# The second token product of an attention and mixer kernel: u by columns at the end of the segment, with x and u turned by DMA

## The chip, the cores and the metric

The kernel runs on one core of a Trainium2 chip. The metric is the device time of one launch in microseconds; smaller is better. The core has five engines with a queue each: TensorE (PE in the profile, with PEld for its weight loads), VectorE (DVE), ScalarE (ACT), GpSimd (POOL) and SyncE (SP), which here only issues DMAs.

## The reference

Cosine attention over 8 batches, 12 heads, 448 positions and 64 columns a head, and then one block of a token and channel mixer on its output. In short (the maximum that is taken off the scores is left out):

```python
q_n = q / (norm(q) + 1e-6);  k_n = k / (norm(k) + 1e-6)
attn = softmax(q_n @ k_n.T / tau)            # per batch and head, 448 x 448
x = (attn @ v) -> (8, 448, 768)              # heads side by side
xt = x.transpose(0, 2, 1)
h = relu(xt @ w_tok1) @ w_tok2               # 448 -> 256 -> 448 positions
u = x + h.transpose(0, 2, 1)
out = u + relu(u @ w_ch1) @ w_ch2            # 768 -> 1536 -> 768 columns
```

## The kernel before, in words

Work goes by **pairs** of heads: 8 batches of 6 pairs make 48, numbered i. Pair i belongs to batch i // 6. Positions of a pair lie in blocks of 128 (448 is three and a half; the half block lies at the end in even batches and at the front in odd ones, with zeros for the other half), 128 columns of a pair beside each other.

The order of all instructions is written out by hand (`manual_schedule`): each engine runs its own list in program order. Pairs 0 to 6 have their own prologue. From pair 7 on the **main loop** runs one **segment** for each i. In a segment i, TensorE does in this order:

- `score(i, 0..2)`: q times k into the banks psS (L340); ScalarE takes the exponential into pt (L341);
- `pv_rest(i - 1)` (L362) and `pv(i - 1)` (L379): pt times v into two banks psO, one for each head; VectorE divides by the row sum and writes x (L382, L383);
- a **unit** of the channel mixer of the batch before: one series of six matmuls into psG (`m_ch1`, L431), which ScalarE turns into gt (L434), or one of twelve into psF (`m_ch2`, L446), to which VectorE adds u (ost, L450);
- `score_rest(i)`: the rest of the scores, psQ (L347);
- `tok2(i - 2)`: the second token product. Eight matmuls of 128 columns (L406) give psU with positions on the partitions, VectorE adds x and writes u (u16, L409), and `udma` turns u by a DMA into ut, columns on the partitions, for `m_ch1` (L415);
- in segments up to 10, `tpose(i + 1)`: q and k of the next pair turned on TensorE (L317, copied out at L319). From pair 12 on this is done two segments ahead by a DMA instead (`tpose_dma`, L325; the bound is `DMA_T0`);
- more units, as many as the list `queue` says are due (`due()`), the first of them with `wide`;
- `tok1(i - 1)`: the first token product into psR (L392); VectorE writes the maximum with 0 as rt (L395).

`side(i)` stands between, with the other engines' work: loads of q and k some seven pairs ahead, squares and casts on GpSimd, norms on ScalarE, scaling of q and k into kq on GpSimd (L293, L301), `tpose_dma(i + 2)`, and the load of v four pairs ahead. From pair 18 on norms are taken for three pairs together. SP's list has, for each segment: q, k (and every third one the rests kr of three pairs), q's and k's transposition, v (and vr), u's transposition, and the stores of the output rows from ost.

The eight accumulation banks are two pools. Pool `ps`, tag b, has two buffers of one bank: psO, psU, psR, psT, pst and units that are not wide take turns in it. Pool `ps2`, tag s, has three of two banks: psS, psQ and wide units. A buffer is handed out again in the order of the program, so an allocation waits for the readers of the one two before it (in ps).

Before the main loop GpSimd sets some buffers to zero, loads the token weights w1t and w2n by DMA (L182, L186) and lays w2n out as w2t (`place_w2`, L189).

After segment 47 come the last pv, two tok2, one tok1, and the units that are left.

Of the kernel before, what the change touches and what calls it, by code (L numbers as in the profile page):

```python
# [7 lines left out]
FP32 = mybir.dt.float32  # L8
FP16 = mybir.dt.float16
AF = mybir.ActivationFunctionType  # L10
ALU = mybir.AluOpType
# [11 lines left out]
def kernel(  # L23
# [12 lines left out]
    nc = tc.nc  # L36

    B, H, S, E = q.shape
# [3 lines left out]
    SC = 112  # L42
    NCH = S // SC
    DT = D // 128
    CT = C // 128
    TT = T // 128
    DH = 384
    NDH = D // DH
    NPAIR = H // 2
# [2 lines left out]
    NHALF = 2 * B  # L52
    inv_tau = 1.0 / float(tau)
    EPS_NORM = 1e-6
    DMA_T0 = 12
    OLD = 2 * NPAIR
    SINGLE = 3 * NPAIR

# [8 lines left out]
    QS = 2 * NCH  # L67
# [16 lines left out]
    cst = ctx.enter_context(tc.tile_pool(name="cst", bufs=1))  # L84
    qkv = ctx.enter_context(tc.tile_pool(name="qkv", bufs=7))
    nrm = ctx.enter_context(tc.tile_pool(name="nrm", bufs=3))
    att = ctx.enter_context(tc.tile_pool(name="att", bufs=4))
    mix = ctx.enter_context(tc.tile_pool(name="mix", bufs=2))
    outp = ctx.enter_context(tc.tile_pool(name="outp", bufs=3))
    ps = ctx.enter_context(tc.tile_pool(name="ps", bufs=2, space=bass.MemoryType.PSUM))  # L90
# [3 lines left out]
    pipe = {}  # L94
    ut = {}
# [53 lines left out]

    w1t = cst.tile([128, 5, T], FP16, name="w1t")  # L150
    w2n = outp.tile([128, TT, S], FP16, name="w2n", tag="ost")
    w2t = cst.tile([128, TT, S + 64], FP16, name="w2t")
    wc1t = cst.tile([128, DT, C], FP16, name="wc1t")
    wc2t = cst.tile([128, CT, D], FP16, name="wc2t")

# [11 lines left out]
        pts.append(pt)  # L167
    nc.gpsimd.memset(w1t[64:128, 3, :], 0.0)
    nc.gpsimd.memset(w1t[0:64, 4, :], 0.0)
    nc.gpsimd.memset(w2t[:, :, S:S + 64], 0.0)  # L170

    def weights_tok1():
        todo = []
# [12 lines left out]
        nc.gpsimd.dma_start(out=w2n[:], in_=moe_w_tok2.rearrange("(tt p) s -> p tt s", p=128))  # L186

    def place_w2():
        nc.gpsimd.tensor_copy(out=w2t[:, :, 0:S].rearrange("p t (c s) -> p t c s", c=NCH),  # L189
                              in_=w2n[:].rearrange("p t (s c) -> p t c s", c=NCH))  # L190

    def weights_ch1(i):
        cols, t = slice(768 * (i // 2), 768 * (i // 2) + 768), 3 * (i % 2)
# [3 lines left out]
    def weights_ch2(i):  # L197
        nc.gpsimd.dma_start(out=wc2t[:, 6 * i:6 * i + 6, :],
                            in_=moe_w_ch2[768 * i:768 * (i + 1)].rearrange("(t p) d -> p t d", p=128))
# [8 lines left out]
    nes = [cst.tile([128, 2 * QS, 2], FP32, name=f"ne{i}") for i in range(3)]  # L208
    for ne in nes:
        nc.vector.memset(ne[:, :, 1], EPS_NORM)  # L210
    for sq in sqs:
        nc.vector.memset(sq[96:128, KS:KS + QS].rearrange("p c e -> p (c e)"), 0.0)

# [38 lines left out]
    def sums_of(i):  # L252
        n, col, w = (-1 - i, 0, 1) if i < SINGLE else (i // HP, i % HP, HP)
        h = half.setdefault(n, {})
        if "ssq" not in h:
            tag = "" if w > 1 else "1"
            h["ssq"] = nrm.tile([128, w, 2 * QS], FP32, name=f"ssq_{i}", tag="ssq" + tag, bufs=4)
            h["rn"] = nrm.tile([128, w, 2 * QS], FP32, name=f"rn_{i}", tag="rn" + tag, bufs=4)
        return h, col

    def sums(i, a0=0, a1=2):
# [90 lines left out]
    def pv_rest(i):  # L352
        if old(i):
            return
        st = pipe[i]
        st["x"] = att.tile([128, 4, 128], FP16, name=f"x_{i}", tag="x", bufs=3)
        st["psO"] = [ps.tile([128, 4, E + 2], FP32, name=f"psO_{i}_{hh}", tag="b") for hh in range(2)]
        for m, lo in enumerate(windows(i // NPAIR)):
            for hh in range(2):
                hb = slice(hh * 64, hh * 64 + 64)  # L360
                at = 2 * S * KC + lo
                nc.tensor.matmul(st["psO"][hh][:, m, 0:E + 1], pts[i % 2][hb, at:at + 128],  # L362
                                 vts[(i // HP) % NV][hb, i % HP, 2 * KC, 0:E + 1], start=(m == 0), stop=False)

    def pv(i, hh):
        st = pipe[i]
        vt = vts[(i // HP) % NV]
        if old(i):
            if hh == 0:
                st["x"] = att.tile([128, 4, 128], FP16, name=f"x_{i}", tag="x", bufs=3)  # L370
            n, nch = SC, NCH
            psO = ps.tile([128, 4, E + 2], FP32, name=f"psO_{i}_{hh}", tag="b")
        else:
            n, nch = 128, KC
            psO = st["psO"][hh]
        for m, lo in enumerate(windows(i // NPAIR)):
            for c in range(nch):
                at = (2 * c + hh) * S + lo
                nc.tensor.matmul(psO[:, m, 0:E + 1], pts[i % 2][0:n, at:at + 128], vt[0:n, i % HP, nch * hh + c, 0:E + 1],  # L379
                                 start=(old(i) and c == 0), stop=(c == nch - 1 and (old(i) or m == 3)))  # L380
        rec = att.tile([128, 4], FP32, name=f"rec_{i}_{hh}", tag="rec")
        nc.vector.reciprocal(out=rec[:], in_=psO[:, :, E])  # L382
        nc.vector.tensor_tensor(out=st["x"][:, :, hh * E:(hh + 1) * E], in0=psO[:, :, 0:E],  # L383
                                in1=_bcast_free(rec[:], E), op=ALU.mult)

    def tok1(i, wide=False):
        st = pipe[i]
        w1 = (0, 1, 2, 3) if (i // NPAIR) % 2 == 0 else (4, 0, 1, 2)
        psR = (ps2 if wide else ps).tile([128, TT, 128], FP32, name=f"psR_{i}", tag="s" if wide else "b")
        for tt in range(TT):  # L390
            for m in range(4):
                nc.tensor.matmul(psR[:, tt], w1t[:, w1[m], tt * 128:(tt + 1) * 128], st["x"][:, m],  # L392
                                 start=(m == 0), stop=(m == 3))
        st["rt"] = att.tile([128, TT, 128], FP16, name=f"rt_{i}", tag="rt", bufs=2)
        nc.vector.tensor_scalar_max(out=st["rt"][:], in0=psR[:], scalar1=0.0)  # L395

    def tok2(i, pe=False, wide=False):
        st = pipe[i]
        b, pj = i // NPAIR, i % NPAIR
        if pj == 0:  # L400
            u16[b] = mix.tile([128, DT, 4, 128], FP16, name=f"u16_{b}", tag="u16", bufs=4)
            ut[b] = mix.tile([128, DT, 4, 128], FP16, name=f"ut_{b}", tag="ut")
        psU = (ps2 if wide else ps).tile([128, 4, 128], FP32, name=f"psU_{i}", tag="s" if wide else "b")
        for m, lo in enumerate(windows(b)):
            for tt in range(TT):
                nc.tensor.matmul(psU[:, m], w2t[:, tt, lo:lo + 128], st["rt"][:, tt],  # L406
                                 start=(tt == 0), stop=(tt == TT - 1))
        u = u16[b][:, pj]
        nc.vector.tensor_tensor(out=u, in0=psU[:], in1=st["x"][:], op=ALU.add)  # L409
        if not pe:  # L410
            udma(i)
# [72 lines left out]
    def unit(wide=False):  # L484
        if queue:
            t, fn = queue.pop(0)
            fn(wide)
            fed[0] -= t
# [14 lines left out]
    with tc.manual_schedule():  # L503
# [119 lines left out]
        def side(i):  # L623
            single = i + 2 < SINGLE
            n = 6 if i < 2 * NPAIR else 7
            for t in range(i + n, i + (8 if i == 2 * NPAIR - 1 else n + 1)):
                if t < NP_ALL:
                    load_qk(t)
            for t in SQ_AT.get(i, [i + 3 if single else i + 5]):
                if t < NP_ALL:  # L630
                    squares(t)
            cast_v(i)
            if i in (8, 10):
                weights_ch2((i - 8) // 2)
            if single:
                norms(i + 2, i + 3)
                norms(i + 2, i + 3, dve=True)
            elif i + 4 < NP_ALL:
                sums(i + 4)
                if (i + 4) % HP == 2:  # L640
                    norms(i + 2, i + 5, act=True)
            if i + 2 < NP_ALL:
                scaled(i + 2)
                if i + 2 >= DMA_T0:
                    tpose_dma(i + 2)
            if i + 4 < NP_ALL:
                load_v(i + 4)

        for i in range(NPAIR + 1, NP_ALL):
            b, pj = i // NPAIR, i % NPAIR  # L650
            for c in range(KC):
                score(i, c)
            pv_rest(i - 1)
            pv(i - 1, 0)
            pv(i - 1, 1)
            if i == NPAIR + 1:
                upose(NPAIR - 2)
                upose(NPAIR - 1)
                refill(0)
            elif pj == 2 and b > 1:  # L660
                refill(b - 1)
            side(i)
            fed[0] += fed[1]
            unit(True)
            if old(i):
                score(i, KC)
            else:
                score_rest(i)
            if i > NPAIR + 1:
                tok2(i - 2)  # L670
            if i + 1 < DMA_T0:
                tpose(i + 1)
            if due():
                unit(True)
            while due():
                unit()
            tok1(i - 1)
            if i + 2 < SINGLE:
                for t in SU_AT.get(i, [i + 3]):
                    sums(t)  # L680
        last = NP_ALL - 1
        pv_rest(last)
        pv(last, 0)
        pv(last, 1)
        tok2(last - 1)
        unit()
        tok1(last)
        unit()
        tok2(last)
        refill(B - 1)  # L690
# [37 lines left out]
```

## Time and profile before

| | |
|---|---|
| runs shown | 397.54 us median of 3 (396.83 to 399.86) |
| the profiled execution | 395.4 us |
| its span (first to last instruction) | 393.6 us |
| PE busy in the span | 375.2 us, 95% |
| ACT, POOL, DVE busy | 224.8, 236.0, 210.5 us |
| DMA queue of SP (q1) | 113104 packets, 67.6% of 16 engines' span |
| L406, psU, 384 matmuls | 29.4 us busy |
| L415, u's transposition | 45 issues, median 3.2 us to landing |
| L325, q's and k's transposition | 36 issues, median 3.4 us to landing |

Busy time of an engine says how long it had work, not whether anything waited for it; matmuls overlap, so their durations in rows add up to more than the time from one to the next. In rows of a timeline the columns are start and duration in us, engine, line and operation, output and inputs, shapes and count, and in brackets the idle time before and what ended it. SPq rows are issues by SP's queue: their duration is how long the queue was held, not the transfer. "Landing" is the transfer's end.

### The profile page before, as it was taken

What the parts mean: (1) busy time and instruction counts of PE and PEld (TensorE: products, weight loads), DVE (VectorE), ACT (ScalarE), POOL (GpSimd) and SP (SyncE); (2) the same over time, 40 slices, a digit from 0 to 9 for tenths busy, and PEclk for the clock granted to TensorE, in tenths of its full rate; (3) what the DMA queues carried; (4) which work ended last, traced back from release to release, by engine and by line L of the source; (5) the groups of instructions that cost most, each with busy time, mean ns of one, the idle gap of its engine ahead of it and who ended that gap; (6) DMA issues with size and microseconds to landing.
All of it is one profiled execution on the core that took longest, in us unless ns stands there. A gap on an engine that the chain in (4) does not pass through costs nothing.

```text
span 393.6 us, 10211 instructions
## 1 busy us (share of the span) xinstructions
PE 375.2 (95%) x4132; PEld 243.5 (62%) x4132; DVE 210.5 (53%) x469; ACT 224.8 (57%) x378; POOL 236.0 (60%) x383
## 2 busy tenths in 40 slices
PE   5899899899999999999999999999999999999994
PEld 5567566476556666667656666667666666655562
DVE  6889767567544574465534574456534653421031
ACT  5899578665574547764574547755575536411400
POOL 6999887889777592939587592949484630000000
PEclk9899999999999999999999999999999999999999
DMA  8999999989787778896897688686786384022022
GB/s 213 260 234 205 243 260 195 219 216 218 177 201 172 156 182 213 161 174 177 176 220 165 156 213 202 159 176 146 183 187 132 91 158 68 15 65 83 0 81 81
DMA packets 117951, 65.26 MB, mean 166 GB/s; under 512 B 75920, under 2 KB 114320, under 8 KB 117904
## 3 DMA queue, kind: packets, MB, share of 16 engines
q1 hardware_dynamic: 113104, 58.71, 67.6%
q0 software_dynamic: 4080, 5.21, 7.7%
q10 hardware_dynamic: 720, 0.69, 0.6%
q8 instruction: 32, 0.52, 0.6%
q14 instruction: 15, 0.12, 0.1%
HBM read 43.45 MB, written 11.01 MB: 138 GB/s over the span
## 4 chain that ended last, share of the span: by engine, by line
PE 79%; POOL 6%; ACT 5%; DVE 5%; issue 2%; DMA 1%; POOLq 0%
PE psF L446 26%; PE psG L431 26%; PE psO L379 8%; PE psS L340 6%; PE psU L406 5%; PE psR L392 4%; ACT pt L341 3%; POOL kq L293 2%; PE psQ L347 2%; POOL sq L241 1%; DVE ssq L264 1%; PE psO L362 1%; POOL w1t L182 1%; DVE ost L450 1%; DMA qk<-kq 1%
## 5 line engine op out<-in xcount | busy, mean ns | idle before, releaser
L341 ACT ACTIVATE pt<-psS 128x896 f16<-128x896 f32 (+1 forms) x156 | 132.5, 917 | 57.8 <-PE psS L340 57.6
L431 PE MATMUL psG<-ut,wc1t 128*128 128x448 f16 x576 | 116.8, 352 | 0.8 <-ACT gt L434 0.8
L446 PE MATMUL psF<-wc2t,gt 128*128 128x384 f16 x672 | 115.9, 326 | 0.2 <-ACT gt L434 0.2
L446 PEld LDWEIGHTS <-gt 128*128 128x128 f16 x672 | 63.6, 98 | 39.0 <-issue 0.3
L434 ACT ACTIVATE gt<-psG 128x448 f16<-128x448 f32 x96 | 51.3, 543 | 60.9 <-PE psG L431 60.9
L293 POOL TENSOR_TENSOR kq<-kf,rn 128x384 f16<-128x384 f32 (+1 forms) x47 | 42.3, 899 | 70.8 <-ACT rn L281 62.0
L431 PEld LDWEIGHTS <-wc1t 128*128 128x128 f16 x576 | 53.9, 98 | 45.4 <-issue 1.1
L450 DVE TENSOR_TENSOR ost<-psF,u 128x384 f32<-128x384 f32 (+1 forms) x64 | 35.5, 554 | 63.6 <-PE psF L446 62.3
L264 DVE TENSOR_REDUCE ssq<-sq 128x15 f32<-128x960 f32 (+2 forms) x49 | 55.7, 1140 | 3.0 <-ACT sq L239 2.9
L395 DVE TENSOR_SCALAR rt<-psR 128x256 f16<-128x256 f32 x48 | 20.2, 420 | 62.6 <-PE psR L392 62.5
L293 POOL TENSOR_TENSOR kq<-qf,rn 112x512 f16<-112x512 f32 x45 | 47.0, 1044 | 3.0
L379 PE MATMUL psO<-vt,pt 128*128 128x65 f16 (+1 forms) x1248 | 48.3, 193 | 0.0
L379 PEld LDWEIGHTS <-pt 128*128 128x128 f16 (+1 forms) x1248 | 42.2, 97 | 5.1 <-issue 1.9
L340 PE MATMUL psS<-qk 64*128 64x448 f16 x312 | 41.3, 358 | 3.5 <-DMA qk<-kq 2.1
L383 DVE TENSOR_TENSOR x<-psO,rec 128x256 f16<-128x256 f32 x96 | 40.8, 425 | 3.3
L241 POOL TENSOR_TENSOR sq<-kf 128x384 f32<-128x384 f32 (+1 forms) x46 | 40.1, 872 | 1.9 <-DVE ssq L264 1.9
L241 POOL TENSOR_TENSOR sq<-qf 112x512 f32<-112x512 f32 x39 | 40.5, 1039 | 0.0
L409 DVE TENSOR_TENSOR u<-psU,x 128x512 f16<-128x512 f32 x48 | 33.0, 688 | 6.0 <-PE psU L406 4.4
L382 DVE RECIPROCAL rec<-psO 128x4 f32<-128x4 f32 x96 | 16.9, 176 | 29.0 <-PE psO L379 29.0
L406 PEld LDWEIGHTS <-w2t 128*128 128x128 f16 x384 | 24.6, 98 | 10.4 <-issue 3.3
L406 PE MATMUL psU<-rt,w2t 128*128 128x128 f16 x384 | 29.4, 219 | 1.7 <-DVE rt L395 1.1
L392 PEld LDWEIGHTS <-w1t 128*128 128x128 f16 x384 | 25.0, 98 | 8.2 <-DVE x L383 1.2
(55 smaller groups left out, 262.2 us busy)
## 6 DMA issues: line engine op xcount, KB each, us to landing
qf<-in_q_dram SPq DMA_DIRECT2D x48, 224.0 KB, 3.9
kf<-in_k_dram SPq DMA_DIRECT2D x36, 192.0 KB, 3.4
vf<-in_v_dram SPq DMA_DIRECT2D x36, 192.0 KB, 3.2
vf<-in_v_dram SPq DMA_DIRECT2D x12, 224.0 KB, 7.8
out_dram<-ost SPq DMA_DIRECT2D x8, 336.0 KB, 3.1
wc1t<-in_moe_w_ch_dram POOLq DMA_DIRECT2D x4, 576.0 KB, 10.2
wc2t<-in_moe_w_ch_dram POOLq DMA_DIRECT2D x2, 1152.0 KB, 10.7
out_dram<-ost SPq DMA_DIRECT2D x8, 288.0 KB, 2.9
```

The source lines that it names most:

```text
L241: nc.gpsimd.tensor_mul(out=dst, in0=src, in1=src)
L264: nc.vector.tensor_reduce(out=h["ssq"][0:n, col, sl], in_=pipe[i]["sq"][0:n, sl], axis=AXX.X, op=ALU.add)
L293: eng.tensor_tensor(out=kq[0:p, a, 0:n].rearrange("p c g e -> p g c e"), in0=st["kq"[a]][:].rearrange("p (g c) e -> p g c e", g=2), in1=_b ...
L340: nc.tensor.matmul(psS[:, hh, 0:S], qk[hb, c * n:c * n + 128], qm[hb], start=True, stop=True)
L341: nc.scalar.activation(out=pts[i % 2][0:n, 2 * S * c:2 * S * (c + 1)].rearrange("p (h s) -> p h s", h=2), in_=psS[0:n, :, 0:S], func=AF.Ex ...
L379: nc.tensor.matmul(psO[:, m, 0:E + 1], pts[i % 2][0:n, at:at + 128], vt[0:n, i % HP, nch * hh + c, 0:E + 1], start=(old(i) and c == 0), st ...
L383: nc.vector.tensor_tensor(out=st["x"][:, :, hh * E:(hh + 1) * E], in0=psO[:, :, 0:E], in1=_bcast_free(rec[:], E), op=ALU.mult)
L392: nc.tensor.matmul(psR[:, tt], w1t[:, w1[m], tt * 128:(tt + 1) * 128], st["x"][:, m], start=(m == 0), stop=(m == 3))
L406: nc.tensor.matmul(psU[:, m], w2t[:, tt, lo:lo + 128], st["rt"][:, tt], start=(tt == 0), stop=(tt == TT - 1))
L431: nc.tensor.matmul(psG[:, 0:S], wc1t[:, dt, ct * 128:(ct + 1) * 128], ut[b][:, dt].rearrange("p m s -> p (m s)")[:, lo:lo + S], start=(dt ...
L434: nc.scalar.activation(out=gt[:, ct, (b % 2) * S:(b % 2 + 1) * S], in_=psG[:, 0:S], func=AF.Relu)
L446: nc.tensor.matmul(psF[:, 0:DH], gt[:, ct, lo:lo + 128], wc2t[:, ct, dh * DH:(dh + 1) * DH], start=(ct == 0), stop=(ct == CT - 1))
```

## The change

- From pair 12 (batch 2) on `tok2` has rt as the stationary operand and w2t as the moving one: two matmuls of 448 columns into psU, columns of u on the partitions. VectorE adds x in that layout and writes ut directly; a DMA turns ut into u16, which `m_ch2` adds.
- For that, x of each of these pairs is turned by a DMA too, `xdma`, into xt. It is issued on SP in the next segment, between the loads of q and k and q's and k's transposition.
- From segment 14 on `tok2(i - 2)` stands at the end of the segment, after the due units and ahead of `tok1(i - 1)`. After the last segment the order is xdma, a unit, tok1, tok2, two units, tok2.
- Pair 12's q and k are turned on TensorE in segment 11.
- ut becomes two fixed buffers, of which GpSimd zeroes a part once; w2t is 64 columns wider with a second small copy; x has two buffers where it had three, and the sums of squares and norms of three pairs have three where they had four.

```diff
-    DMA_T0 = 12
+    DMA_T0 = 13
...
-    w2t = cst.tile([128, TT, S + 64], FP16, name="w2t")
+    w2t = cst.tile([128, TT, S + 128], FP16, name="w2t")
...
-    nc.gpsimd.memset(w2t[:, :, S:S + 64], 0.0)
+    nc.gpsimd.memset(w2t[:, :, S + 64:S + 128], 0.0)
...
+        w2c = w2n[:].rearrange("p t (s c) -> p t c s", c=NCH)
+        nc.gpsimd.tensor_copy(out=w2t[:, :, 64:S + 64].rearrange("p t (c s) -> p t c s", c=NCH), in_=w2c)
+        nc.gpsimd.tensor_copy(out=w2t[:, :, 0:64], in_=w2c[:, :, NCH - 1, SC - 64:SC])
...
+    uts = [cst.tile([128, DT, 4, 128], FP16, name=f"ut{i}") for i in range(2)]
+    for i in range(2):
+        nc.gpsimd.memset(uts[i][:, :, 3 - 3 * i, 64 - 64 * i:128 - 64 * i], 0.0)
...
-        st["x"] = att.tile([128, 4, 128], FP16, name=f"x_{i}", tag="x", bufs=3)
+        st["x"] = att.tile([128, 4, 128], FP16, name=f"x_{i}", tag="x", bufs=2)
...
+    def xdma(i):
+        st = pipe[i]
+        st["xt"] = att.tile([128, 4, 128], FP16, name=f"xt_{i}", tag="xt", bufs=2)
+        nc.sync.dma_start_transpose(out=st["xt"][:], in_=st["x"][:].rearrange("p m d -> p (m d)"))
...
     def tok2(i, pe=False, wide=False):
...
-            ut[b] = mix.tile([128, DT, 4, 128], FP16, name=f"ut_{b}", tag="ut")
+            ut[b] = uts[b % 2]
+        if i >= OLD:
+            lo = 64 * (b % 2)
+            psU = ps.tile([128, 512], FP32, name=f"psU_{i}", tag="b")
+            for tt in range(TT):
+                nc.tensor.matmul(psU[:, 0:S], st["rt"][:, tt], w2t[:, tt, 64 - lo:64 - lo + S],
+                                 start=(tt == 0), stop=(tt == TT - 1))
+            nc.vector.tensor_tensor(out=ut[b][:, pj].rearrange("p m s -> p (m s)")[:, lo:lo + S], in0=psU[:, 0:S],
+                                    in1=st["xt"].rearrange("p m s -> p (m s)")[:, lo:lo + S], op=ALU.add)
+            nc.sync.dma_start_transpose(out=u16[b][:, pj], in_=ut[b][:, pj].rearrange("p m s -> p (m s)"))
+            return
...
+            if i > OLD:
+                xdma(i - 1)
...
-            if i > NPAIR + 1:
+            if NPAIR + 1 < i < OLD + 2:
                 tok2(i - 2)
...
             while due():
                 unit()
+            if i >= OLD + 2:
+                tok2(i - 2)
             tok1(i - 1)
...
+        xdma(last)
+        unit()
+        tok1(last)
         tok2(last - 1)
         unit()
-        tok1(last)
         unit()
         tok2(last)
```

More of the change, by code (lines that the diff above doesn't have):

```diff
@@ L188, in place_w2 @@
     def place_w2():
-        nc.gpsimd.tensor_copy(out=w2t[:, :, 0:S].rearrange("p t (c s) -> p t c s", c=NCH),
-                              in_=w2n[:].rearrange("p t (s c) -> p t c s", c=NCH))
+        w2c = w2n[:].rearrange("p t (s c) -> p t c s", c=NCH)
+        nc.gpsimd.tensor_copy(out=w2t[:, :, 64:S + 64].rearrange("p t (c s) -> p t c s", c=NCH), in_=w2c)
+        nc.gpsimd.tensor_copy(out=w2t[:, :, 0:64], in_=w2c[:, :, NCH - 1, SC - 64:SC])
     def weights_ch1(i):
@@ L256, in sums_of @@
             tag = "" if w > 1 else "1"
-            h["ssq"] = nrm.tile([128, w, 2 * QS], FP32, name=f"ssq_{i}", tag="ssq" + tag, bufs=4)
-            h["rn"] = nrm.tile([128, w, 2 * QS], FP32, name=f"rn_{i}", tag="rn" + tag, bufs=4)
+            h["ssq"] = nrm.tile([128, w, 2 * QS], FP32, name=f"ssq_{i}", tag="ssq" + tag, bufs=3 + (w == 1))
+            h["rn"] = nrm.tile([128, w, 2 * QS], FP32, name=f"rn_{i}", tag="rn" + tag, bufs=3 + (w == 1))
         return h, col
@@ L369, in pv @@
             if hh == 0:
-                st["x"] = att.tile([128, 4, 128], FP16, name=f"x_{i}", tag="x", bufs=3)
+                st["x"] = att.tile([128, 4, 128], FP16, name=f"x_{i}", tag="x", bufs=2)
             n, nch = SC, NCH
@@ L405, in tok2 @@
             for tt in range(TT):
-                nc.tensor.matmul(psU[:, m], w2t[:, tt, lo:lo + 128], st["rt"][:, tt],
+                nc.tensor.matmul(psU[:, m], w2t[:, tt, 64 + lo:64 + lo + 128], st["rt"][:, tt],
                                  start=(tt == 0), stop=(tt == TT - 1))
```

## The prediction

> **What bounds the kernel now.** I read the page first: the slices of the span and the chain that ended last.
>
> ```profile
> PE   5899899899999999999999999999999999999994
> PEclk9899999999999999999999999999999999999999
> DMA  8999999989787778896897688686786384022022
> PE 79%; POOL 6%; ACT 5%; DVE 5%; issue 2%; DMA 1%; POOLq 0%
> ```
>
> TensorE is nine tenths busy from the third slice on, at full granted clock, and carries 79% of the chain. "Busy" alone could hide idling, so next come the stretches of three segments (a segment: one pass of the main loop, one pair of heads; columns: stretch, then PE, PEld, DVE, ACT, POOL, the clock, DMA share, GB/s).
>
> ```profile
> 157.56:178.44 20.88, 20.88 (x240) 13.65 (x239) 11.07 (x24) 13.41 (x23) 14.47 (x26) 1.00 0.90 169
> 201.59:224.09 22.50, 22.50 (x252) 14.88 (x251) 12.28 (x26) 12.48 (x21) 15.28 (x27) 1.00 0.75 176
> ```
>
> PE fills the stretches to the last hundredth. So a microsecond that TensorE must wait in segments 14 to 47 is added to the time, whatever engine it waits for. Then the timeline of one segment, to see the margins around the two token products:
>
> ```profile
> 213.00 2.11 PE L446 MATMUL psF<-wc2t,gt 128*128 128x384 f16 x12
> 214.95 0.61 PE L392 MATMUL psR<-x,w1t 128*128 128x128 f16 x8
> 215.15 0.56 DVE L450 TENSOR_TENSOR ost<-psF,u 128x384 f32<-128x384 f32 x1 [1.26 <-PE psF L446]
> 215.49 0.74 PE L340 MATMUL psS<-qk 64*128 64x448 f16 x6
> 215.62 0.41 DVE L395 TENSOR_SCALAR rt<-psR 128x256 f16<-128x256 f32 x1
> 216.07 0.30 PE L362 MATMUL psO<-vt,pt 64*128 64x65 f16 x8
> ```
>
> L362's second output takes the bank that L395 empties; L395 ends at 216.03, L362 starts at 216.07. That margin is nothing. Last, the one place (the tail) where a series follows the bank's previous owner with only one short series between:
>
> ```profile
> 344.82 0.61 PE L392 MATMUL psR<-x,w1t 128*128 128x128 f16 x8
> 345.02 0.54 ACT L434 ACTIVATE gt<-psG 128x448 f16<-128x448 f32 x1 [3.77 <-PE psG L431]
> 345.62 1.29 PE L431 MATMUL psG<-ut,wc1t 128*128 128x448 f16 x6 [0.18 <-ACT gt L434]
> ```
>
> The earlier psG is issued out at 344.82, where psR starts; its bank is free for the next series at 345.62. From the last issue of a series to its bank's reuse it takes **0.80 us** (0.20 until ScalarE starts, 0.54, 0.06).
>
> **The change, part by part.** The sum is made against the profiled execution, 395.4 us (span 393.6 and 1.8 around it); the median shown, 397.54, lies 2.1 above it.
>
> *Shape of the second product.* 36 pairs (12 to 47). Before: eight matmuls of 128 columns, from psU at 212.55 to the next series at 213.00, 0.45. After: two of 448 columns; psG's six of that width take 1.14 in the chain, so 0.19 each, 0.38. Saved 0.07 x 36 = **-2.5**.
>
> *Its place.* psU now stands after the due units, directly ahead of psR. Pool ps has two buffers under tag b, handed out in turn: psO0, psO1, units beyond the first due one, psU, psR. psR therefore takes the buffer of the last such unit, with only psU's 0.38 between, where before a whole unit (1.14 or 1.95) stood there. By the 0.80 above, TensorE waits 0.80 - 0.38 = 0.42. Behind psR in its queue stand the next segment's scores, and ScalarE waits for those. Counting the order of allocations in segments 14 to 47, 23 have such a unit; 0.42 x 23 = **+9.7**. Lower end: the profile calls the idle time in that row 0.18 (it counts from a modelled end), x 23 = 4.1; I take 0.42, since issue to issue is what the segment's length is made of.
>
> *The other 11 segments.* psR takes psO1's buffer, free long before. But VectorE now has, in this order, ost, the addition, and rt, all within the margin seen above. With the rows of that segment: ost to 215.71, the addition from 215.62 (VectorE starts one about 0.08 before the last ends) for 0.62 (between 0.56 for 384 and 0.69 for 512 columns) to 216.24, rt to 216.57, reuse 0.05 later, 216.62; L362's second output is due at 216.07 + 0.38 = 216.45. Waiting 0.18 x 11 = **+2.0**; ends 0 (the addition early) and 0.4 each (two ost of one unit ahead of it).
>
> *SP's queue.* The new transposition of x is issued on SP, once a segment from 13 on, ahead of q's and k's transposition for two pairs later.
>
> ```profile
> 202.14 0.59 SPq L111 DMA_DIRECT2D vf<-in_v_dram  x1
> 202.82 1.19 SPq L415 DMA_TRANSPOSE ut<-u  x1
> 204.05 0.58 SPq L129 DMA_DIRECT2D qf<-in_q_dram  x1
> 204.68 0.46 SPq L111 DMA_DIRECT2D kf<-in_k_dram  x1
> 205.18 1.29 SPq L119 DMA_DIRECT2D kr<-in_k_dram  x2
> 206.58 1.26 SPq L325 DMA_TRANSPOSE qk<-kq  x1
> ```
>
> This queue is nearly solid: a transposition of this size holds it 1.19, 1.27 with what lies beside it. Its idle time is that ahead of every third L325, where kq comes late: 1.6, 3.4, 1.5, 4.3, 0.9, 4.0, 3.3, 3.9 and 0.6 between 112 and 289 us, 23 in all. Up to pair 42's L325, 29 issues of 1.27 are added, 37. That leaves it 14 later; pair 42's q and k land 4.7 ahead of their use (288.96, landed 292.3, used 296.98), and 1.6 is won early where L325 for pair 12 is gone. So SP alone would delay the end by about 8. TensorE's own delay by segment 42 is 19 x 0.35 + 9 x 0.11 + 0.4 = 8.0. The two are level: SP hides behind TensorE by a hair. I add **+0.8** for pairs 23, 26 and 38, which land only 2 to 3.5 ahead; ends 0 and the second case below. The issue itself waits for x (L383), done some 2 us into a segment, long before SP gets there; behind it stand q's, k's and v's. VectorE's addition waits for the turned x, with rt behind it, but only a segment later, when q and k issued after it have landed, so it is late only if these are. u's transposition now goes out later by two to four units; u's rows are wanted a batch later, no cost. The 36 transfers move 512 packets each; at the queue's mean of 38 ns a packet (67.6% of 16 x 393.6 over 113104) that is at most 1.2 us of all 16 engines in a segment of 7.3, on a share of 0.72 to 0.90. Between 63 and 90 us the share was 1.06, so there is room, at the price of later landings.
>
> *Start and pair 12.* GpSimd gets two memsets (about 0.4 each by 0.20 for 128 and 0.31 for 256 columns) and a second copy into w2t (0.2). The memsets are partly hidden by its 2.5 wait for w1t's landing and 0.55 before its first kq: 0.3 comes through, and the copy: +0.5. Eight transposes for pair 12 (0.5 on PE, one copy on VectorE) end the wait of 1.9 before psS at 77.49, some -1.5. But pair 14's scores wait for kq from a GpSimd that runs without a gap from 76 to 91, so that gain is stood out again. Together **+0.4**, ends -1.9 and +1.0.
>
> Sum: 395.4 - 2.5 + 9.7 + 2.0 + 0.8 + 0.4 = 405.8, and on the median 2.1 more, 407.9: **408 us**. The fewer x and ssq buffers cost nothing: x's old reader is done a segment before, and only two ssq of three pairs live at once.
>
> The Trainium skill's "Perfetto Trace Analysis", section "Matmuls", says that larger matmuls are more efficient, and that independent groups should rotate through PSUM banks so that an eviction overlaps the next group. The first half speaks for the change and would give 395.4 - 2.5 = 392.9; the second speaks against its place. The rows above show both, 0.07 and 0.42, so the second decides.
>
> "Advanced Engine Details and Errata", section "X-Bar Transpose (TRN2)", says that transposing DMAs are as fast as regular ones. On SP's queue the rows say otherwise: 1.2 against 0.46 to 0.59. By the page 29 issues would cost 18, less than the 23 of idle time, and SP could not bind.
>
> **The rivals.** *SP's queue binds.* Issues get stretched at times (2.42 for one at 209.88); the mean of L415 in steady state is 1.38, with its surroundings 1.47. Then 29 x 1.47 - 23 - 4.7 - 1.6 = 13.3 at pair 42, and 1.6 on TensorE from there on: 395.4 + 13.3 + 1.6 = 410.3, 412 on the median. For it: the high DMA share; against: the qk landings have 2 to 6 us in hand.
>
> *The other side: TensorE never waits for the bank.* If the eviction came within 0.45 of the last issue instead of 0.80, psR would find its buffer free, the shorter product would count in full, and pair 12's wait could stay won: 395.4 - 2.5 - 1.5 = 391.4, 393.5 on the median. It decides where the row of 0.18 idle is absent from segments 14 on. Against it stand the row above and a second like it (psG issued out at 340.50, its bank reused at 341.30).
>
> *Half price.* TensorE loses only the 0.18 that the profile calls idle and the 11 segments lose nothing: 395.4 - 2.5 + 4.1 + 0.4 = 397.4, 399.5 on the median.
>
> **How the numbers follow.** Forecast 0.57; SP binds 0.20; other side 0.12; half price 0.11. About 1% either way can be told from no change here (393.6 to 401.5). Slower by more: the first two, 0.77. Same: half price and a third of the other side, 0.15; faster 0.08. The range goes from just under half price, 398, to 415, which is SP's case with its landings late by another 2 to 3.
>
> **What would show it.** In the profile after: idle time of TensorE ahead of psR put down to ACT gt (18 segments) and DVE ost (5), about 0.2 a row, none before; psU x2 taking 0.38; PE short of its stretches by one to two us in each three segments. SP right: its idle time ahead of every third qk gone or nearly, few waits of psS for DMA; many such waits or x's DMA waited for by VectorE mean the SP case. I am wrong if psR shows no wait.

## The result, and the profile after

The changed kernel takes 412.0 us (median of 4, 409.9 to 414.27) beside 398.7 for the kernel before in the same runs: ratio 1.034, 95% interval 1.025 to 1.043. The profiled execution takes 409.9 with a span of 407.7, against 395.4 and 393.6: 14.1 longer. The prediction was 408, in a range of 398 to 415.

The slices of the span and the chain that ended last, from the page of the kernel after:

```profile
PE   5899899989989999999999999999999999999995
PEclk9899999999999999999999999999999999999999
DMA  8999999999897989899896979869889684133023
PE 62%; POOL 9%; ACT 9%; DVE 7%; DMA 6%; issue 3%; SPq 2%; POOLq 0%
```

The clock is the same. TensorE carries 62% of the chain where it carried 79%; DMAs, ScalarE, GpSimd and VectorE have what it lost. The same three-segment stretches as before (columns: stretch, then PE, PEld, DVE, ACT, POOL, the clock, DMA share, GB/s):

```profile
161.64:183.35 21.71, 21.19 (x221) 12.87 (x220) 10.91 (x25) 13.22 (x22) 13.91 (x24) 1.00 0.92 176
207.84:231.25 23.41, 22.88 (x234) 14.06 (x233) 12.20 (x26) 12.29 (x20) 14.95 (x26) 1.00 0.94 177
```

PE no longer fills them: 0.52 and 0.53 are missing, though the stretches grew by 0.83 and 0.91. "Idle" is counted from a modelled end of the last matmul, so it shows only part of what a wait costs. The timeline of the end of a segment shows the wait itself:

```profile
212.73 1.68 PE L454 MATMUL psG<-ut,wc1t 128*128 128x448 f16 x8
214.24 0.54 PE L420 MATMUL psU<-w2t,rt 128*128 128x448 f16 x2
214.44 0.54 ACT L457 ACTIVATE gt<-psG 128x448 f16<-128x448 f32 x1 [0.59 <-PE psG L454]
214.82 0.62 DVE L422 TENSOR_TENSOR ut<-psU,xt 128x448 f16<-128x448 f32 x1 [3.34 <-PE psU L420]
215.03 0.61 PE L398 MATMUL psR<-x,w1t 128*128 128x128 f16 x8 [0.26 <-ACT gt L457]
215.68 0.42 DVE L401 TENSOR_SCALAR rt<-psR 128x256 f16<-128x256 f32 x1 [0.24 <-PE psR L398]
```

The last psG is issued out at 214.24, where psU starts; psR starts at 215.03, 0.79 later, after ScalarE has emptied that psG's bank (214.44 to 214.98). Two matmuls of 448 columns would have taken 0.38. In the page's rows of the whole run, psR and the scores look like this (last column: idle time just before, and what ended most of it):

```profile
L398 PE MATMUL psR<-x,w1t 128*128 128x128 f16 x384 | 29.2, 219 | 5.5 <-ACT gt L457 4.1
L346 PE MATMUL psS<-qk 64*128 64x448 f16 x312 | 40.9, 357 | 4.6 <-DMA qk<-kq 4.2
```

And SP's queue in one of these segments:

```profile
205.40 1.20 SPq L424 DMA_TRANSPOSE u<-ut  x1
206.65 0.82 SPq L129 DMA_DIRECT2D qf<-in_q_dram  x1
207.53 0.47 SPq L111 DMA_DIRECT2D kf<-in_k_dram  x1
208.09 1.19 SPq L406 DMA_TRANSPOSE xt<-x  x1
209.39 1.25 SPq L331 DMA_TRANSPOSE qk<-kq  x1
210.69 0.59 SPq L111 DMA_DIRECT2D vf<-in_v_dram  x1
211.38 1.19 SPq L424 DMA_TRANSPOSE u<-ut  x1
```

Each row starts within 0.11 us of the end of the one before it. Between 100 and 290 us SP's idle stretches of over 0.3 us add up to 0.9; in the kernel before they added up to 24.1.

**Where the 14.1 lies.** A series is the run of matmuls that fills one bank (or pair of banks), such as psU's two. For every series I took the time from its start to the next one's start, less its own issue time (the same span where nothing waits), over the 33 segments from the start of pair 14 to the start of pair 47. They take 258.25 where they took 244.57.

| from pair 14 to pair 47 | us |
|---|---|
| psU's issue, 0.45 to 0.38 | -2.3 |
| psR after psU, 0.40 on the mean of 22 segments | +8.8 |
| scores that wait for q and k to land | +2.9 |
| waits inside the units and ahead of psU | +1.6 |
| the wide unit behind psQ | +1.4 |
| L368's second output, behind rt | +1.0 |
| rest | +0.2 |
| difference | +13.7 |

Pair 14 starts 0.4 late, and 0.4 + 13.7 is the 14.1.

By this table the wait for psR's bank (the row "psR after psU") makes up two thirds. The question for the experiments was whether it is also the cause: whether the time comes down when the wait is taken away. **Theory A**: it does, the place decides. **Theory B**: SP's queue, now solid, sets the end, and the bank wait only fills time in which TensorE would otherwise wait for q and k.

### The profile page after: what moved, and what is told of

Same layout as the page of the kernel before. It is cut to its first block, busy times and chain, and to the rows that moved or that the text cites. A ratio compares the mean times of both kernels' runs of the same rounds, so it can differ in the third digit from the quotient of the medians.

```text
span 407.7 us, 9917 instructions
## 1 busy us (share of the span) xinstructions
PE 380.1 (93%) x3924; PEld 234.6 (58%) x3924; DVE 209.0 (51%) x470; ACT 224.8 (55%) x378; POOL 237.3 (58%) x386
## 4 chain that ended last, share of the span: by engine, by line
PE 62%; POOL 9%; ACT 9%; DVE 7%; DMA 6%; issue 3%; SPq 2%; POOLq 0%
PE psF L469 21%; PE psG L454 20%; PE psO L385 7%; PE psS L346 6%; DMA qk<-kq 4%; PE psR L398 4%; ACT gt L457 3%; POOL kq L299 3%; ACT pt L347 3%; POOL sq L247 3%; DVE ssq L270 2%; DVE x L389 1%; DVE ost L473 1%; PE psO L368 1%; PE psQ L353 1%
## 5 line engine op out<-in xcount | busy, mean ns | idle before, releaser
L422 DVE TENSOR_TENSOR ut<-psU,xt 128x448 f16<-128x448 f32 x36 | 22.4, 621 | 63.4 <-PE psU L420 59.2
L398 PEld LDWEIGHTS <-w1t 128*128 128x128 f16 x384 | 24.9, 97 | 18.1 <-issue 11.7
L398 PE MATMUL psR<-x,w1t 128*128 128x128 f16 x384 | 29.2, 219 | 5.5 <-ACT gt L457 4.1
L354 ACT ACTIVATE pt<-psQ 128x448 f16<-128x448 f32 x36 | 19.4, 539 | 17.7 <-PE psQ L353 17.7
```

## The experiments

Each run stands beside runs of the kernel before on the same chip; ratios are to those. "Segments" is the time from the start of pair 14 to the start of pair 47 in the run's profile (244.6 before, 258.3 after).

**1. psU in another bank.** The new psU leaves the pool whose buffers psR and the units share.

```diff
-            psU = ps.tile([128, 512], FP32, name=f"psU_{i}", tag="b")
+            psU = ps2.tile([128, 512], FP32, name=f"psU_{i}", tag="s")
```

> The kernel after, but the new psU takes its bank from pool ps2 instead of ps, so that psR gets the bank of two allocations back. If the bank rotation is the cause, the 0.40 between psU's end and psR is gone in all 22 segments that show it in the profile after, 8.8 together: the profiled execution falls from 409.9 by 7 to 9, to 401 to 403, and the ratio to before is 1.01 to 1.02. If SP's queue is what binds (its own delay was put at 8 by pair 42), taking the wait away lets TensorE run into late q and k: idle time of psS behind the DMA grows from 4 percent of the chain by as much as the wait gave, and the execution stays at 407 to 410.

Ratio 1.027 (1.021 to 1.034), profiled execution 408.2, segments 257.7. The same place in the segment:

```profile
213.25 0.54 PE L454 MATMUL psG<-ut,wc1t 128*128 128x448 f16 x2
213.63 0.54 PE L420 MATMUL psU<-w2t,rt 128*128 128x448 f16 x2
214.01 0.61 PE L398 MATMUL psR<-x,w1t 128*128 128x128 f16 x8
215.30 0.74 PE L346 MATMUL psS<-qk 64*128 64x448 f16 x6 [0.68 <-DMA qk<-kq]
```

The bank wait is gone, psU to psR takes 0.38 everywhere. One series later TensorE stands still again, until q and k have landed: the summary of qk's reads by TensorE says

```profile
  DMA qk<-kq: 12.2, 15
```

(us, times) where the kernel after has 4.2 in 5. Of the 8.8 that the wait took, 0.5 came back. Theory A alone does not hold.

**2. No transposition of x.** So is it SP?

```diff
-            if i > OLD:
-                xdma(i - 1)
...
-                                    in1=st["xt"].rearrange("p m s -> p (m s)")[:, lo:lo + S], op=ALU.add)
+                                    in1=st["x"].rearrange("p m s -> p (m s)")[:, lo:lo + S], op=ALU.add)
```

> The kernel after without the transposition of x: the addition reads x as it lies, so x's part of u is not turned (x keeps three buffers, as before). If the waits of psS for q and k (2.9 in segments 14 to 46 of the profile after) come from x's issues on SP, they go, and the rest stays: 409.9 - 3 = 406 to 408. If SP binds, the gain is 6 or more, to 404 or less; if x's issues cost nothing, it stays within 1 of 409.9.

Ratio 1.030 (1.025 to 1.035), profiled execution 408.0, segments 255.7. The waits for q and k in these segments fall from 2.9 to 0.2, and that is all. The bank wait is 8.8 as in the kernel after; what psR waited for (us, times), 4.1 in 16 for ScalarE there too:

```profile
  ACT gt L453: 4.1, 16
  DVE ost L469: 1.3, 5
```

Theory B alone does not hold either.

**3. Each cause put into the kernel before, alone.** First the place: the old product of eight matmuls, moved to the end of the segment.

```diff
-            if i > NPAIR + 1:
+            if NPAIR + 1 < i < OLD + 2:
                 tok2(i - 2)
...
             while due():
                 unit()
+            if i >= OLD + 2:
+                tok2(i - 2)
             tok1(i - 1)
```

> The kernel before with one edit: from batch 2 on the second token product, in its old form of eight matmuls and with u still turned by a transposition, stands after the due units, directly ahead of psR. No transposition of x. If the place is the cause: 0.80 - 0.45 = 0.35 of waiting for psR in 22 or 23 segments, about 8, with 1 to 3 from rt behind the addition and from units that now follow the exponential sooner: profiled execution 395.4 + 9 to 11 = 404 to 407, ratio about 1.025. If the transposition of x on SP is what costs, this kernel has nothing of it and stays within 395 to 398.

Ratio 1.031 (1.026 to 1.037). Segments 256.5, +11.9: 7.3 of it is the wait behind psU, and most of the rest the small waits of the table above (1.6 inside the units and ahead of psU, 1.3 behind psQ, 1.6 behind rt), 4.5 where 1 to 3 was expected. The profiled execution, 411.7, also lost 3.9 ahead of pair 14, where the granted clock was 0.50 between 78 and 84 us; without that it would be 407.9, against the expected 404 to 407.

```profile
217.55 0.61 PE L406 MATMUL psU<-rt,w2t 128*128 128x128 f16 x8
218.34 0.61 PE L392 MATMUL psR<-x,w1t 128*128 128x128 f16 x8 [0.19 <-ACT gt L434]
78.00:84.00 6.00, 5.19 (x45) 3.09 (x46) 1.55 (x6) 2.94 (x5) 4.66 (x9) 0.50 1.16 294
```

From psU's start to psR's it is 0.79 again, with a product of 0.45 in between instead of 0.38: the time until the bank is emptied counts here, not the length of the product.

Then SP: the transposition of x, which nobody reads.

```diff
+            if i > OLD:
+                xdma(i - 1)
```

> The kernel before with the transposition of x issued on SP once a segment, at the same place in SP's queue as in the kernel after; nobody reads its output, and everything else stays (the sums of squares get one buffer fewer, to make room). If SP's queue would delay the end by about 8 by itself, as the sum in the prediction has it, TensorE now waits for late q and k ahead of psS, growing from segment 20 on: profiled execution 401 to 404. If the queue has room after all, it stays at 395 to 397.

Ratio 1.031 (1.024 to 1.037), profiled execution 407.4, segments 257.2. TensorE's order is untouched, psR never waits for a bank, and the pairs' starts fall behind all the same: 0.3 at pair 20, 2.4 at 25, 5.3 at 30, 7.8 at 35, 11.7 at 40, 12.4 from 41 on.

```profile
290.85 0.61 PE L392 MATMUL psR<-x,w1t 128*128 128x128 f16 x8
293.01 0.74 PE L340 MATMUL psS<-qk 64*128 64x448 f16 x6 [1.55 <-DMA qk<-kq]
```

So there are **two causes of about the same size**, 11.9 and 12.6 in these segments, each enough by itself.

**4. Both taken away.** Experiments 1 and 2 in one kernel.

> Both edits at once on the kernel after: psU in pool ps2's bank, and no transposition of x (the addition reads x as it lies, so x's part of u is not turned). If the bank wait (8.8) and SP's queue (12.4 by itself) are two causes of about the same size, each hiding the other, taking away both gives what neither gave: about 395.4 - 2.3 (shape) + 1.0 (rt behind the addition) + 1.1 (units that follow the exponential sooner) + 1.6 (waits inside the units and ahead of psU) + 0.4 to 1.5 early = 397 to 399, ratio about 1.005. If there is a third cause beneath them, it stays at 402 or above.

Ratio 1.005 (1.002 to 1.009), profiled execution 398.0, segments 247.9, and the chain is TensorE's again:

```profile
PE 77%; POOL 6%; DVE 6%; ACT 6%; DMA 3%; issue 2%; SPq 0%; POOLq 0%
```

| segments, us | x turned on SP | x not turned |
|---|---|---|
| psU in psR's pool | 258.3 (after) | 255.7 (experiment 2) |
| psU in the other pool | 257.7 (experiment 1) | 247.9 (this) |

Down the right column the bank costs 7.8, along the lower row SP costs 9.8; in the presence of the other they cost 0.5 and 2.5. As I read it, they overlap because a TensorE that waits for one gives the other that time to catch up.

**5. The shape alone.** The new product at the old place, x not turned. Of the change only the shape, the early part and u's transposition are left.

> The kernel after with the new product at the old place, and no transposition of x (the addition reads x as it lies, so x's part of u is not turned): of the change only the shape, the early part and u's transposition after the addition are left. If the shape is worth what its two rows say, 0.07 in each of 36 pairs, segments 14 to 46 take 244.6 - 2.3 = 242.3, and the execution 395.4 - 2.5 + 0.4 = 393.3, ratio 0.993 to 0.997. Against the run with both causes taken away (1.0054) it also gives the price of the new place without its bank wait: 5.5 in segments 14 to 46. If the shape is worth nothing, 1.000; if the new place costs no more than its bank, the two runs agree.

Profiled execution 392.9, segments 242.7, that is 1.9 below the kernel before; ratio 0.989 (0.984 to 0.995).

```profile
211.58 0.35 PE L353 MATMUL psQ<-qk 128*128 128x448 f16 x1
211.77 0.54 PE L416 MATMUL psU<-w2t,rt 128*128 128x448 f16 x2
212.14 2.11 PE L465 MATMUL psF<-wc2t,gt 128*128 128x384 f16 x12
214.09 0.61 PE L398 MATMUL psR<-x,w1t 128*128 128x128 f16 x8
```

psU takes 0.37, with a whole unit between it and psR. Experiment 4 less this one is 5.3: that is the price of the new place when the bank wait is already gone. L368's second output behind rt makes 2.5 of it, the waits inside the units ahead of psU 1.2, the values product behind the third exponential (psS to psO) 1.2, the unit behind psQ 0.3.

**6. What of SP's load binds: issues, bytes or the kind of transfer?** In the kernel of the second half of experiment 3, a plain copy of x in place of its transposition.

```diff
-        nc.sync.dma_start_transpose(out=st["xt"][:], in_=st["x"][:].rearrange("p m d -> p (m d)"))
+        nc.sync.dma_start(out=st["xt"][:], in_=st["x"][:])
```

> The kernel before with a plain copy of x, 128x512, issued on SP where the earlier run issued a transposition of it (nobody reads the copy; the sums of squares get one buffer fewer). Same bytes, same count, another kind of transfer. If what SP loses is the 1.2 that a transposition holds the queue, against 0.5 to 0.6 of a plain transfer, 34 x 0.6 = 20 fits into the 23 of idle time: 395 to 399. If the count of transfers or the bytes bind, it is near the transposition's 407.

Ratio 0.999 (0.996 to 1.002). First the issues of x in that earlier kernel, then in this one (least, median and most time in ns that one held SP's queue):

```profile
L400 SPq DMA_TRANSPOSE xt<-x x36: 1188/1209/2786, 90.5 to 356.0; - x36
```

```profile
L400 SPq DMA_DIRECT2D xt<-x x36: 465/524/1553, 90.7 to 344.6; - x36
```

For the same bytes between the same buffers the medians are 1.21 and 0.52 us. The plain copies leave SP 4.6 of its 24.1 idle, the transpositions 0.8; the scores wait 0.7 for q and k in these segments with the copies, 13.0 with the transpositions. The load of the DMA engines does not explain it: from pair 14 to pair 47 their busy share was 0.88 with the copies and 0.86 with the transpositions.

Then, in the kernel of experiment 1, u turned back three pairs at a time, with everything computed:

```diff
-            nc.sync.dma_start_transpose(out=u16[b][:, pj], in_=ut[b][:, pj].rearrange("p m s -> p (m s)"))
+            if pj % 3 == 2:
+                nc.sync.dma_start_transpose(out=u16[b][:, pj - 2:pj + 1].rearrange("p j m d -> p (j m) d"),
+                                            in_=ut[b][:, pj - 2:pj + 1].rearrange("p j m s -> p (j m s)"))
             return
```

> The kernel after with psU in pool ps2's bank and u turned back three pairs at a time: everything is computed, the place is the new one, and SP has 24 issues fewer. Against the run with the bank alone (407 to 408) only the count of issues changes. If the issues are what makes q and k late, their waits (11.4 in segments 14 to 46) go and the time is that of the run without x's transposition, about 400, ratio 1.004 to 1.008. If the moved bytes are, it stays at 406 or above.

Ratio 1.005 (1.002 to 1.008), segments 248.6: as in experiment 4, with the same bytes moved as in the kernel after, and with the addition waiting for the turned x as there. The views show u's issues (ns, least, median, most) and the scores' waits for q and k in the whole run, which were 12.2 in experiment 1:

```profile
L425 SPq DMA_TRANSPOSE u<-ut x12: 1423/1891/2514, 116.0 to 353.7; - x12
  DMA qk<-kq: 2.2, 2
```

The DMA engines' share from pair 14 to pair 47 is 0.87, as in experiment 1. So what binds is the time that issues hold SP's queue.

**7. Pair 12 by DMA again** (`DMA_T0 = 12` in the kernel after).

> The kernel after with pair 12's q and k turned by DMA again, as before. The wait of 1.9 ahead of pair 12's scores comes back, the eight transposes on TensorE (0.5) go, and pair 13 is no longer waited for: by pair 14 it is within 0.5 of the kernel after, and the profiled execution within 1 of 409.9. If the turn on TensorE was a real gain that something else ate, 411 to 412.

Profiled execution 409.6, against 409.9 for the kernel after; pair 14 starts 0.3 later, pair 47 0.2 earlier. Nothing can be seen that the turn on TensorE gains or costs, as summed.

**8. The old place, all computed.** The kernel after with its product back behind psQ:

> The kernel after with the new product back at the old place, behind psQ and ahead of the second wide unit; x still turned by SP. The bank wait and the small waits of the new place go, so only SP's queue is left, as where x's transposition was added to the kernel before: 395.4 + 12 - 2 = 404 to 407, with idle time of psS behind q and k, and some of VectorE's addition behind x's landing, which has now one unit less of time. If place is all that matters, 393 to 396.

Ratio 1.037 (1.031 to 1.043), segments 260.1: worse than expected, because x is the first to be late there. Of xt in its trace:

```profile
  DMA xt<-x: 35.8, 21
  PE psG L454: 11.2, 8
```

VectorE's addition stands 35.8 us in 21 segments for x's landing, and a unit (second line, who waited for the addition) or psR stands behind psU's bank. The profile is longer for the clock too: between 8 and 30 us it was 0.77, and pair 14 starts 2.2 later than in the kernel after; inside the segments it was 0.50 for 3.4 us twice, from 163.7 and 303.6, by estimate at most 3.4 of the 260.1 (half of these 6.8). That the version is no faster than the kernel after rests on the timed runs.

With u turned three pairs at a time as well:

> A version meant to keep the gain: product of 448 columns at the old place, and u turned back three pairs at a time, one transposition of 128x1536 in place of three of 128x512. In the traces the transposition of 128x1024 for q and k holds SP's queue 1.24, as long as one of 128x512, so what holds it is the issue and not the size: 24 issues fewer take back 30 of the 43 that x's 34 issues cost, and the rest (13) fits into the 23 of idle time. Then TensorE binds again: 395.4 - 2.3 + 0.4 = 393 to 394.5, ratio 0.995. If it is the moved data that makes q and k late, not the issues, it stays at 403 or above; if x lands too late for the old place, psU's bank and rt make it 396 to 400.

Ratio 1.002 (0.998 to 1.006), segments 248.1. SP has room again, but x still lands late in 8 segments:

```profile
  DMA xt<-x: 12.9, 8
  PE psG L456: 4.9, 5
```

So x got one segment more, and the product of pair i - 3 is taken:

```diff
             if NPAIR + 1 < i < OLD + 2:
                 tok2(i - 2)
+            elif i >= OLD + 3:
+                tok2(i - 3)
...
-            elif pj == 2 and b > 1:
+            elif b > 1 and pj == (2 if b == 2 else 3):
                 refill(b - 1)
```

> The version with u turned three pairs at a time and the product at the old place, but with one segment more for x's landing: in segment i the product of pair i - 3 instead of i - 2 (its batch's units are queued a segment later, x's turn and rt get a third buffer, u's rows three buffers instead of four). In the version before it VectorE's addition waited 12.9 for x in 8 segments, and TensorE lost about 5 behind it. If that was all it lost, the shape's 2.3 stands out now: segments 14 to 46 in 242 to 243.5 against 244.6 before, ratio 0.992 to 0.997. If the segment more brings new waits (a segment without units where ScalarE binds), 1.000 or above.

Ratio 0.9965 (0.9938 to 0.9992), 395.84 against 397.57: the only version here that computes everything and has its interval below 1. VectorE never waits for x in it. Its profile doesn't show a gain: from pair 14 to the end it takes 304.9, the kernel before 304.4. Its segments take 240.5, but four units and one psU fewer fall into them (4.9), so the like of 244.6 is 245.4: the shape's 2.3 are there, and 2.8 of waits for q and k in four segments eat them. So the gain rests on the timed runs alone, and an interval that ends at 0.9992, in one of thirteen kernels tried, is not proof of it.

## Why the prediction was right, and where it was not

The direction held, the time lies near the forecast, and the wait that it put first is there as described. But taking that wait away gives almost nothing back, and the size came out near partly by luck, as errors of both signs met. By its steps:

- *Shape*, -2.5 in 36 pairs: 2.3 in the 33 segments summed, and 1.9 net when it stands alone (experiment 5, 392.9 against a sum of 393.3). Right.
- *Bank*, +9.7, 0.42 in 23 segments: 8.8, namely 0.42 to 0.43 in 20 segments and 0.18 in two, where psU itself had already waited 0.24. The lower end, 0.18 a row, was refuted: the row says 0.26 idle, but from issue to issue 0.41 is lost.
- *The other 11 segments*, +2.0: 1.0. The wait is there, and 0.17 in a segment where 0.18 was summed, but it is new in six segments only.
- *Start and pair 12*, +0.4: 0.4. The 1.5 won ahead of pair 12 is there and is lost again by the start of pair 13, as summed. The exact 0.4 is luck: in the other profiles with the same start and a granted clock of 1.00 from 14 us on, pair 14 starts 0.0 to 1.5 late.
- *SP*, +0.8: 2.9. The mis-sized term is the 1.27 for an issue, 1.19 of hold and 0.08 beside it. The hold alone of x's transpositions was 1.34 on the mean between 100 and 290 us in the kernel after, and 1.45 where x's transposition was put into the kernel before (experiment 3); SP's delay by itself was 12.4 there, at pair 42 and to the end, and not 8. The rival "SP's queue binds" had taken 1.47, and its 13.3 was near the delay that SP makes alone.
- *Left out*: the product was moved from between psQ and the second wide unit. So that unit now comes 0.45 sooner after the exponentials and waits for a bank there (1.4), and the units and psU behind it wait for ScalarE (1.6). The sum had priced what stands at the new place and nothing at the one left empty. 3.0 for that and 2.1 for SP, less 1.9 for the bank and the other 11 segments, and 0.9 more in small terms, make up the 4.1 between the 405.8 of the sum and 409.9.

"The two are level: SP hides behind TensorE by a hair" was the sentence that mattered most. That they came out level is in part luck, since both were summed too small: from pair 14 to pair 42 TensorE alone (experiment 2) lost 9.8 where the sum has 7.6, and SP alone (experiment 3) 12.6 where it has 8. And it had a consequence that the prediction didn't draw: no single term of the sum is the gain of undoing it. 9.7 for the bank was nearly right as a row and worth 0.5 as a cure. Its sign of being wrong, no wait ahead of psR, could not have told that: the wait stands in the profile while SP's queue sets nearly the same end.

The Trainium skill's "Perfetto Trace Analysis", section "Matmuls", was weighed as right in both halves, and both showed: the larger product gains 1.9 (experiment 5), and the place where its neighbour cannot rotate through the banks loses 7.8 (right column of experiment 4).

"Advanced Engine Details and Errata", section "X-Bar Transpose (TRN2)", says that transposing DMAs are as fast as regular ones. The landings agree nearly (median 3.4 from issue for x's transposition, 3.1 for its copy), the queue does not: 1.21 against 0.52 of SP for the same bytes, and a ratio of 1.031 against 0.999.

## What to carry to other kernels

When two resources are near their limits, a profile shows the wait of whichever comes first, and taking that one away only uncovers the other: sum each one's delay by itself, put each alone into the old kernel, and expect little gain before both are gone. Count a queue by how long its issues hold it, not by bytes, and turn several tiles with one transposition where nobody needs them soon. When a step is moved, price the gap that it leaves as well as the place to which it goes.

## What the runs showed of the hardware beyond that

The time that a transposition holds SP's queue grows less than its size: medians near 1.2 us for 128x512 and 1.24 for 128x1024 (16-bit), and 1.5 to 2.0 for 128x1536, against three times 1.2; the least were 1.19, 1.23 and 1.41. For 128x1536 that is more than I had expected from the first two.

The granted clock early in an execution is not the same from one execution to the next. Between 8 and 30 us (columns as in the stretches above, the clock third from the end) the kernel after had the first line. The second is of the version of experiment 8 with the product of pair i - 2 and u turned by threes; its work is the same up to there, and its pair 2 started 4.1 later:

```profile
8.00:30.00 22.00, 19.17 (x286) 13.45 (x287) 18.23 (x42) 19.10 (x33) 19.23 (x23) 0.92 1.18 245
```

```profile
8.00:30.00 22.00, 18.41 (x232) 12.75 (x232) 18.14 (x33) 15.84 (x27) 16.07 (x20) 0.77 1.13 233
```

At pair 14 it is still 2.0 later. That is as much as some of the differences in this study, and why the profiles are compared from pair 14 on. From there to pair 47 the granted clock was 1.00 in every profile but that of the first version in experiment 8.
